# A ConvNeXt-V2 block on one core: convolution in two bursts, another set-up order, Gram and bias add moved

## The chip, the cores and the metric

The kernel runs on one core of one Trainium2 chip. The metric is the device time of that core, in microseconds (us), as the median of several executions. Every run has a state; all runs told here are of state "fast", so no number below compares a disturbed run with an undisturbed one. Engines: PE is TensorE (matmul), ACT is ScalarE, DVE is VectorE, POOL is GpSimd, SP is SyncE. Times inside a kernel come from one profiled execution and count from the start of its span.

## The reference, cut to what matters

```python
# x (1,512,512,96), dw (3,3,96), w1 (96,384), w2 (384,96), gamma, beta (384): bfloat16
out = 0
for i in range(3):
    for j in range(3):
        out += xp[:, i:i+H, j:j+W, :] * dw[i, j]           # depthwise convolution, xp is x padded
h = layernorm(out)                                         # over the 96 channels
h = gelu(einsum('bhwc,ce->bhwe', h, w1))                   # expand 96 -> 384, tanh approximation
gx = sqrt((h * h).sum(axis=(1, 2)) + 1e-6)                 # over ALL pixels
nx = gx / (gx.mean(axis=-1) + 1e-6)
h = gamma * (h * nx) + beta + h
return x + einsum('bhwe,ec->bhwc', h, w2)
```

`gx` needs a sum over the whole picture, so the kernel goes over it twice. The first pass (128 blocks of four rows) makes the convolution, the layer norm, the expansion and the sums of squares. Then comes a short chain that turns the sums into a scale for `w2`. The last stage makes the expansion again in part (`gr`), multiplies by the scaled `w2` and writes the output.

## The kernel before

One slot of the first pass convolves a new block `s` and expands an older block `b`. PE makes the convolution in three bursts of 24 matmuls each. (In the timelines below, `stats` are the 24 matmuls of four columns that sum for the layer norm; the Gram matmuls multiply `gm` by itself, and the diagonal of the result holds sums of squares.) The expansion has six units of 1024 columns: three `pair`, which ACT turns into `gsh`, and three `rest`, which ACT turns into `gm`. All six take their tile of PSUM, the memory that matmuls write to, from one pool of two buffers (`psU`, `bufs=2`), in the order in which they are issued.

```python
def pair(j):                       # two 512-column matmuls, then Gelu on ACT
    U = psU.tile([128, 2, QW], f32, name="U")
    ...
    act.activation(out=gsh[:, :, j, :], in_=U[:], func=ACTF.Gelu_apprx_tanh)

def rest(n):                       # matmuls into 1024 columns, then Gelu on ACT
    U = psU.tile([128, 2, QW], f32, name="U")
    ...
    act.activation(out=gms[b][:, c0:end], in_=Uf, func=ACTF.Gelu_apprx_tanh)

# ... one steady slot, in program order:
for f in bursts[0]: f()            # PE: 24 matmuls of the convolution
pair(0)
pair(1)
squares(0)                         # DVE statistics
for f in bursts[1]: f()
turn_x(s + 2)                      # DVE transposes
pair(2)
rest(0)
squares(1)
for f in bursts[2]: f()
evac()                             # ACT: y_bf, the convolution's result out of PSUM
squares(2)
rest(1)
rest(2)
squares_rest()
stage_stats(b2)                    # PE: 24 tiny matmuls, sums for the layer norm
for f in grams: f()                # PE: 12 Gram matmuls, or 24 for every third block
# ... (loops over lists written on one line here)
```

After the first pass, POOL adds `x` and the constant row `B2c` into `xb`. `B2c` is a copy that DVE makes as the last operation of its scale chain:

```python
m2 = ...                           # DVE: some twenty operations on at most 33 columns follow
...
dve2.tensor_scalar(out=W2s[:, j, :], in0=w2_sb[:, j, :], scalar1=sc[:, j:j + 1], ...)
dve2.tensor_copy(out=B2c[:], in_=B2bc_f[:])
stage_xb(ORDER[0])                 # POOL: xb = xr + B2c
```

## Time and profile before

| | us |
|---|---|
| time, median of three runs | 1584.29 (1584.08 to 1584.38) |
| span of the profiled run | 1588.2 |

The page of the profile gives the busy time of each engine, then the span in 40 equal slices. A digit is the busy share in tenths; the row of PE is shown.

```profile
PE 1483.1 (93%) x23719; PEld 851.6 (54%) x23719; DVE 1147.1 (72%) x2056; ACT 1453.0 (91%) x1307; POOL 1310.6 (83%) x920
...
PE   5798999999999999999999997789999999999998
```

PE and ACT are both nearly full, and that alone says nothing about which one limits. Cutting the span into its stages says more. The following lines are the view by stretches of the kernel before: the stretch, its length, the busy time of each engine with its number of instructions, then the mean granted clock, the DMA share and GB/s. (The granted clock is a share of TensorE's full clock, as the profile records it.) The stretches are the ramp, the steady slots, the tail (expansion without convolution), the bridge (the scale chain) and the last stage.

```profile
0.00:126.17 126.17, 91.26 (x1892) 39.80 (x1893) 77.27 (x189) 73.33 (x69) 48.99 (x56) 0.87 0.48 140
126.17:957.46 831.29, 796.42 (x14010) 396.49 (x14009) 711.81 (x1207) 774.23 (x770) 733.48 (x546) 1.00 0.76 233
957.46:1034.38 76.92, 56.01 (x462) 31.88 (x462) 64.72 (x108) 72.92 (x80) 38.01 (x29) 1.00 0.82 253
1034.38:1055.64 21.26, 15.50 (x146) 10.57 (x146) 12.76 (x45) 11.53 (x14) 8.23 (x5) 0.84 0.33 119
1055.64:1588.20 532.56, 523.93 (x7215) 372.84 (x7211) 280.55 (x507) 521.02 (x378) 481.89 (x287) 1.00 0.99 394
```

The steady stretch has a clock of 1.00, and both PE (96%) and ACT (93%) are nearly always at work in it. In the last stage the DMA share is 0.99, but that does not make DMA its limit: ACT's `gr` follow each other with a single wait, 1.5 us before the first of them, and 83% of the stage's chain that ended last is `gr`, so here ACT sets the length. One steady slot of PE, from the timeline of the kernel before (start, length, engine, line, operation, out<-in, count; idle before and its releaser in brackets):

```profile
707.39 0.44 PE L31 MATMUL SG<-rowsel,y_bf 128*128 128x4 bf16 x12
707.69 0.44 PE L31 MATMUL SG<-rowsel,ysq 128*128 128x4 bf16 x12
707.99 0.83 PE L31 MATMUL SG<-gm 128*128 128x128 bf16 x12
708.75 0.87 PE L31 MATMUL Y<-xT,Wq 64*32 64x512 bf16 x24
709.55 1.11 PE L31 MATMUL U<-ynT,w1p 128*128 128x512 bf16 x4
710.77 0.89 PE L31 MATMUL Y<-xT,Wq 64*32 64x512 bf16 x24
711.60 0.60 PE L31 MATMUL U<-ynT,w1p 128*128 128x512 bf16 x2
712.23 0.60 PE L31 MATMUL U<-w1p,ynT 128*128 128x384 bf16 x4
712.94 0.87 PE L31 MATMUL Y<-xT,Wq 64*32 64x512 bf16 x24
713.74 1.08 PE L31 MATMUL U<-w1p,ynT 128*128 128x128 bf16 x8
```

PE has no pause that the timeline marks: stats, Gram, burst, two pairs, burst, third pair, first rest, burst, the other two rests. ACT in the same slot:

```profile
708.08 1.95 ACT L31 ACTIVATE gm<-U 128x1024 bf16<-128x1024 f32 x2
710.24 3.02 ACT L31 ACTIVATE gsh<-U 128x1024 bf16<-128x1024 f32 x3 [0.22 <-ACT gm L31]
713.16 1.02 ACT L31 ACTIVATE gm<-U 128x1024 bf16<-128x1024 f32 x1
714.06 1.46 ACT L31 ACTIVATE y_bf<-Y 128x1536 bf16<-128x1536 f32 x1
715.39 1.96 ACT L31 ACTIVATE gm<-U 128x1024 bf16<-128x1024 f32 x2
```

ACT makes one `gm` ahead of `y_bf` and two behind it, and it waits 0.22 us for the first pair of a slot. The distance from one `y_bf` to the next is 7.32 us, or 7.87 us for every third block, with 24 Gram matmuls.

### The profile page before, as it was taken

What the parts mean: (1) busy time and instruction counts of PE and PEld (TensorE: products, weight loads), DVE (VectorE), ACT (ScalarE), POOL (GpSimd) and SP (SyncE); (2) the same over time, 40 slices, a digit from 0 to 9 for tenths busy, and PEclk for the clock granted to TensorE, in tenths of its full rate; (3) what the DMA queues carried; (4) which work ended last, traced back from release to release, by engine and by line L of the source; (5) the groups of instructions that cost most, each with busy time, mean ns of one, the idle gap of its engine ahead of it and who ended that gap; (6) DMA issues with size and microseconds to landing.
All of it is one profiled execution on the core that took longest, in us unless ns stands there. A gap on an engine that the chain in (4) does not pass through costs nothing. (4 is left out here: it accounts for less than half of the span.)

```text
span 1588.2 us, 55647 instructions
## 1 busy us (share of the span) xinstructions
PE 1483.1 (93%) x23719; PEld 851.6 (54%) x23719; DVE 1147.1 (72%) x2056; ACT 1453.0 (91%) x1307; POOL 1310.6 (83%) x920
## 2 busy tenths in 40 slices
PE   5798999999999999999999997789999999999998
PEld 1343454444454444444445444457777777777776
DVE  7746888878888888888888888955555555555554
ACT  3777999988999999999999999979999999999998
POOL 0457898897889899898989887369999999899997
PEclk7899999999999999999999999999999999999999
DMA  3549677777778868777877858869999999999995
GB/s 107 164 128 284 210 237 250 220 227 214 252 217 242 264 215 244 231 242 221 250 235 239 245 176 239 249 223 415 410 404 409 410 408 407 411 412 409 412 409 234
DMA packets 186366, 443.67 MB, mean 279 GB/s; under 512 B 33958, under 2 KB 83206, under 8 KB 186118
## 3 DMA queue, kind: packets, MB, share of 16 engines
q1 hardware_dynamic: 171156, 373.10, 69.7%
q0 software_dynamic: 13600, 66.86, 10.7%
q8 instruction: 186, 3.05, 0.8%
q14 instruction: 62, 0.51, 0.1%
q10 hardware_dynamic: 1362, 0.15, 0.1%
HBM read 289.30 MB, written 150.72 MB: 277 GB/s over the span
## 5 line engine op out<-in xcount | busy, mean ns | idle before, releaser
L31 PE MATMUL U<-ynT,w1p 128*128 128x512 bf16 x2166 | 613.4, 382 | 28.5 <-ACT gsh L31 12.1
L31 DVE BATCH_NORM_STATS2 bst<-gsh 128x6 f32<-128x512 bf16 x756 | 468.0, 673 | 142.8 <-ACT gsh L31 142.8
L31 ACT ACTIVATE gr<-U 128x1536 bf16<-128x1536 f32 (+1 forms) x384 | 526.9, 1444 | 15.2 <-PE U L31 9.7
L31 DVE TENSOR_TENSOR o_sb<-O,xb 128x384 bf16<-128x384 f32 x512 | 283.2, 557 | 254.1 <-PE O L31 214.4
L31 POOL TENSOR_TENSOR yn<-y_bf,rbc 128x1536 bf16<-128x1536 bf16 x128 | 397.3, 3107 | 75.8 <-ACT rbc L31 45.0
L31 ACT ACTIVATE gsh<-U 128x1024 bf16<-128x1024 f32 x378 | 370.7, 1023 | 70.5 <-ACT gm L31 44.8
L739 POOL TENSOR_TENSOR xb<-xr,B2c 128x1536 f32<-128x1536 bf16 x128 | 400.8, 3133 | 41.1 <-DVE B2c L31 38.7
L31 ACT ACTIVATE gm<-U 128x1024 bf16<-128x1024 f32 x384 | 379.4, 1039 | 0.1
L31 PE MATMUL Y<-xT,Wq 64*32 64x511 bf16 (+1 forms) x8694 | 326.6, 391 | 29.8 <-issue 3.0
L31 POOL TENSOR_TENSOR ysq<-y_bf 128x1536 bf16<-128x1536 bf16 x114 | 313.5, 2750 | 48.0 <-ACT y_bf L31 47.8
L31 PEld LDWEIGHTS <-w1p 128*128 128x128 bf16 x2166 | 171.7, 98 | 286.7 <-issue 191.7
L31 PEld LDWEIGHTS <-gr 128*128 128x128 bf16 x4584 | 241.5, 98 | 113.1 <-ACT gr L31 13.5
L31 PE MATMUL O<-W2s,gr 128*128 128x96 bf16 x4584 | 279.0, 207 | 5.3 <-DVE o_sb L31 0.8
L31 PEld LDWEIGHTS <-Wq 64*32 64x32 bf16 x9216 | 106.4, 91 | 211.1 <-issue 165.5
L31 ACT ACTIVATE y_bf<-Y 128x1536 bf16<-128x1536 f32 x121 | 176.2, 1456 | 17.1 <-PE Y L31 16.9
L31 DVE STREAM_TRANSPOSE xT<-xin 128x576 f32<-128x576 f32 (+1 forms) x256 | 181.2, 747 | 0.0
L31 PE MATMUL U<-w1p,ynT 128*128 128x384 bf16 (+2 forms) x1032 | 148.4, 273 | 10.7 <-ACT gm L31 4.7
L31 DVE BATCH_NORM_STATS2 bst<-gm 128x6 f32<-128x512 bf16 x252 | 156.8, 677 | 0.7 <-ACT gm L31 0.6
L31 PE MATMUL SG<-gm 128*128 128x128 bf16 x2064 | 135.6, 219 | 0.0
L31 PEld LDWEIGHTS <-ynT 128*128 128x128 bf16 x1032 | 91.3, 97 | 82.4 <-issue 48.1
L31 PEld LDWEIGHTS <-gm 128*128 128x128 bf16 x2064 | 117.3, 97 | 0.9
L714 POOL DMA_DIRECT2D xr<-in_x_dram x128 | 71.0, 555 | 37.9 <-POOL xb L739 34.7
(97 smaller groups left out, 687.8 us busy)
## 6 DMA issues: line engine op xcount, KB each, us to landing
ynT<-yn_dram SPq DMA_DIRECT2D x126, 512.0 KB
xin<-in_x_dram SPq DMA_DIRECT2D x126, 432.0 KB
yn_dram<-yn SPq DMA_DIRECT2D x512, 96.0 KB
ynT<-yn_dram SPq DMA_DIRECT2D x128, 384.0 KB
xr<-in_x_dram POOLq DMA_DIRECT2D x128, 384.0 KB, 6.5
out_dram<-o_sb SPq DMA_DIRECT2D x128, 384.0 KB
g_dram<-gsh SPq DMA_DIRECT2D x126, 384.0 KB
gl<-g_dram SPq DMA_DIRECT2D x84, 384.0 KB
```

The lines of the kernel that those rows point to most:

```text
L31: r = f(*a, **k)
L714: nc.gpsimd.dma_start(out=xr[:], in_=x[0, r0:r0 + GR].rearrange("r w c -> (r w) c").rearrange("(p g) c -> p g c", g=PXP))
L739: nc.gpsimd.tensor_tensor(out=xb[:], in0=grp[q]["xr"][:], in1=B2c[:, None, :].to_broadcast([128, PXP, C]), op=ALU.add)
```

## The change

The intent: fewer switches of PE between convolution and expansion (two bursts instead of three), a set-up that brings the first convolution earlier and gives PE matmuls that nobody reads, in the hope of a higher granted clock, Gram sums that keep PE busy where it used to wait, and a bias add that runs beside the scale chain and not behind it. The core of the diff:

```diff
-    for n in (1, 1, 1, 1):                      # batches of the layer norm in the ramp
+    for n in (1, 1, 2):
@@ set-up
+        for t in yn_ring:                       # six fills, from DVE memset to ACT
+            act.activation(out=t[C:128, :, :], in_=zrow[C:128, None, :]..., func=ACTF.Identity)
+        pool.memset(Wq[:], 0.0)                 # was dve
+        busy(FILL[0])                           # 6, later 24 matmuls that nobody reads
...     # late_setup() of DVE is cut in three: setup_stats(), setup_mlp() at the end of
...     # slot 2, setup_rest() at the end of slot 4
@@ one steady slot
+            bursts = [taps[:2], taps[2:]]
                 for f in bursts[0]:
                     f()
+                if not taps:                    # tail: Gram of the previous block here
+                    for b2 in get("gram"):
+                        if b2 != b:
+                            gram_mms(b2)
                 pair(0)
                 pair(1)
                 squares(0)
                 spread_out()
-                for f in bursts[1]:
-                    f()
                 if s + 2 < NBLK:
                     turn_x(s + 2)
                 pair(2)
-                rest(0)
                 squares(1)
...
-                for f in bursts[2]:
+                for f in bursts[1]:
                     f()
                 if evac:
                     evac()
+                rest(0)
                 squares(2)
                 rest(1)
                 rest(2)
@@ behind the first pass
-        LEAD = UPB
+        LEAD = 2 * UPB                          # six gr ahead of the chain, not three
         advance(LEAD, PRE)
+        stage_xb(ORDER[0])                      # ahead of the chain
...
-        dve2.tensor_copy(out=B2c[:], in_=B2bc_f[:])
-        stage_xb(ORDER[0])
@@ stage_xb
-                                    in1=B2c[:, None, :].to_broadcast([128, PXP, C]), op=ALU.add)
+                                    in1=B2bc_f[:, None, :].to_broadcast([128, PXP, C]), op=ALU.add)
```

## The prediction

> **What bounds the kernel now.** Span 1588.2 us, three stages (timeline, stretches).
> - Ramp, to about 125 us: set-up, granted clock 0.57 to 0.66 between 20 and 60 us, first expansion (ACT gsh) at 53.2 us, steady expansions from 126 us.
> - Steady blocks, to 957 us. ACT does three gsh (0.93 us pitch), three gm (0.93) and y_bf (1.34): 7.0 us a block. Block periods are 7.22 us, and 7.85 for every third block (24 Gram matmuls, not 12); mean with hiccups 7.55 over 107 blocks. Not ACT alone: at each boundary it waits 0.2 or 0.83 us (PE comes late with the first pair).
> - Tail without convolution (5.6 us a block), a bridge (1040 to 1056; ACT busy 10.3 of 20 us), then expansions gr back to back on ACT (1.38 us each, 99% busy).

> **The loop that matters.** Expansions rotate over two PSUM tiles; the sixth (last rest) overwrites the tile that the first gm reads. So: first gsh starts -> first gm ends (3.83 us) -> last rest (0.53) -> stats (0.61) -> Gram (0.76 or 1.43) -> conv burst (0.80) -> first pair until its gsh starts (0.69). Sum 7.22 or 7.89: the measured periods.

> **What the change does to it.** New order, PE: two bursts, three pairs, third burst, three rests, stats, Gram; ACT: gsh x3, y_bf, gm x3.
> 1. y_bf precedes the first gm: +1.34 us in the loop.
> 2. The second burst precedes the first pair: three back-to-back bursts take 2.78 us, so +0.98.
> The saved switch between convolution and expansion (0.1 to 0.3 us of PE) falls where PE waits for the first gm anyway. Period 9.5 and 10.2 us: +2.3 on some 110 blocks (part hidden in hiccups): **+246 us**.
> 3. Tail: Gram of the previous block precedes the next pairs and needs the last gm, so ACT waits Gram plus 0.76 us: +1.45 us on 14 blocks, less 1.4 us of Gram at the end: **+19 us**.
> 4. Ramp: DVE loses 5.4 us of ynT memsets and half the Wq copies; the second convolution no longer waits until 21.7 us[...]. But ACT fills ynT, six writes of 1.9 us (estimate from the 1536-element ysq, 1.48 us), so the first y_bf stays near 18 us. First gsh near 42 us; then early blocks are slower and one more conv-only slot (3.6 us) comes. Net **-9 us**.
> 5. Bridge: six expansions before the scale chain, not three, fill 2.6 us of ACT wait; xb (3.1 us) leaves the chain; but they delay the tot matmul by 1.8 us, and the longer lead leaves four more output groups at the end. Net **-4 us**.

> **Prediction:** 1584.3 + 246 + 19 - 9 - 4 = about **1836 us**, 8 in 10 between 1790 and 1880. Faster by over 2%: 0.02; within 2%: 0.02; slower by over 2%: 0.96.

> **Right if:** period 9.4 to 10.3 us; ACT idle 2 to 2.5 us before each first gsh; PE idle about 1.5 us before each last rest, released by the first gm; PE busy 75 to 85% in the steady stretch, clock 1.00; tail blocks 7.05/7.75 us; first gsh at 36 to 46 us; last stage unchanged.
> **Wrong if:** the last rest need not wait for the first gm; PE gaps lower the clock (slower still); the ramp gains tens of us.

## The result, and the profile after

| kernel | median, us | lowest to highest | runs |
|---|---|---|---|
| before | 1584.34 | 1584.08 to 1587.6 | 4 |
| after | 1899.84 | 1898.48 to 1900.22 | 4 |

The ratio of after to before is 1.1984, 95% interval 1.1963 to 1.2005. A ratio here is the mean time of one kernel's fast runs over that of the other's of the same rounds, so it is not quite the ratio of the medians that are quoted. The direction was predicted, and the time lies 64 us above the predicted 1836 and above the upper end, 1880.

The same lines of the page of the kernel after:

```profile
PE 1528.9 (81%) x23749; PEld 905.5 (48%) x23749; DVE 1141.3 (60%) x2026; ACT 1451.8 (76%) x1312; POOL 1314.1 (69%) x927
...
PE   6777777777777777777777777776699999999998
```

ACT and DVE do the same work within 0.6%, and PE is busy 46 us longer although the change adds only the thirty fill matmuls. Part of the work must have run slower. The view by stretches, cut at the same events:

```profile
0.00:125.91 125.91, 92.02 (x1850) 41.48 (x1851) 63.12 (x158) 80.73 (x71) 47.10 (x50) 0.89 0.45 132
125.91:1251.27 1125.36, 846.50 (x14096) 448.43 (x14095) 715.63 (x1209) 771.71 (x773) 744.22 (x561) 0.95 0.58 175
1251.27:1342.21 90.94, 60.27 (x475) 33.12 (x474) 64.81 (x108) 72.86 (x79) 32.66 (x26) 0.98 0.66 213
1342.21:1365.90 23.69, 10.88 (x72) 5.89 (x71) 19.57 (x40) 11.21 (x12) 10.87 (x6) 0.81 0.34 112
1365.90:1898.40 532.50, 519.24 (x7263) 376.61 (x7260) 278.13 (x511) 515.30 (x378) 479.29 (x285) 1.00 0.98 392
```

Subtracting the lengths gives the ledger:

| stage | before | after | difference | predicted |
|---|---|---|---|---|
| ramp | 126.17 | 125.91 | -0.3 | -9 |
| steady | 831.29 | 1125.36 | +294.1 | +246 |
| tail | 76.92 | 90.94 | +14.0 | +19 |
| bridge | 21.26 | 23.69 | +2.4 | -4 |
| last stage | 532.56 | 532.50 | -0.1 | 0 |
| sum | 1588.2 | 1898.4 | +310.2 | +252 |

(The cuts in both kernels are the first `gsh` of the steady slots, the first `gsh` after the last `y_bf`, the last expansion into `resg`, which is the `gsh` of the two blocks kept on chip, and the seventh `gr`. The steady stretch of after holds one more slot of convolution alone, 4 to 5 us, which the prediction had booked under the ramp.) The steady stage is nearly all of it. PE in two of its slots in the kernel after:

```profile
704.74 0.60 PE L32 MATMUL U<-w1p,ynT 128*128 128x256 bf16 x4 [1.60 <-ACT gm L32]
...
705.78 0.83 PE L32 MATMUL SG<-gm 128*128 128x128 bf16 x12
706.54 1.86 PE L32 MATMUL Y<-xT,Wq 64*32 64x512 bf16 x48
708.33 1.04 PE L32 MATMUL U<-ynT,w1p 128*128 128x512 bf16 x4
710.10 0.59 PE L32 MATMUL U<-ynT,w1p 128*128 128x512 bf16 x2 [0.73 <-ACT gsh L32]
...
714.25 0.60 PE L32 MATMUL U<-w1p,ynT 128*128 128x256 bf16 x4 [1.60 <-ACT gm L32]
...
715.28 2.72 PE L32 MATMUL SG<-gm 128*128 128x128 bf16 x24
717.93 2.23 PE L32 MATMUL Y<-xT,Wq 64*32 64x512 bf16 x48
```

The first slot is what the prediction described: the last rest waits 1.60 us for the first `gm`, and then stats, 12 Gram matmuls (0.83), two bursts (1.86) and the first pair follow each other. In the second slot 24 Gram matmuls take 2.72 us. They took 1.50 us in the kernel before (at 700.09 us of its timeline), and the two bursts take 2.23 and not 1.86 us. ACT, in the same stretch of the kernel after, shows what this costs:

```profile
709.02 2.85 ACT L32 ACTIVATE gsh<-U 128x1024 bf16<-128x1024 f32 x3 [2.50 <-issue]
711.83 1.45 ACT L32 ACTIVATE y_bf<-Y 128x1536 bf16<-128x1536 f32 x1
713.18 2.85 ACT L32 ACTIVATE gm<-U 128x1024 bf16<-128x1024 f32 x3
720.79 2.85 ACT L32 ACTIVATE gsh<-U 128x1024 bf16<-128x1024 f32 x3 [4.75 <-issue]
```

(`<-issue` means that the profile shows nothing that the engine waited for.) ACT idles 2.50 us ahead of a normal slot, as predicted (2 to 2.5), and 4.75 us ahead of a third one. `y_bf` follows `y_bf` at 9.5, 9.5 and 11.75 us. Predicted were 9.5 and 10.2. The reason is the granted clock, the third column from the right in the view by stretches, here in pieces of 3.4 us of the kernel after:

```profile
708.40:711.80 3.40, 2.57 (x31) 0.82 (x32) 1.72 (x3) 2.78 (x3) 3.40 (x2) 1.00 0.41 102
711.80:715.20 3.40, 1.80 (x30) 1.25 (x29) 3.40 (x8) 3.40 (x5) 3.40 (x2) 1.00 0.46 134
715.20:718.60 3.40, 3.40 (x49) 2.84 (x54) 1.76 (x3) 0.83 (x1) 3.40 (x2) 0.52 0.74 209
718.60:722.00 3.40, 2.54 (x45) 0.78 (x30) 0.16 (x1) 1.21 (x2) 1.29 (x1) 0.98 0.93 290
```

The clock falls to half for one such piece, just when the longest run of PE work begins. The piece before it has PE busy for 1.80 of 3.40 us, and 0.6 us of that are the tiny stats matmuls of four columns. By the clock records of the trace, falls begin at 715.3, 746.0, 776.8, 807.5, 838.2 and 868.9 us, 30.72 us apart, which is three slots (9.5 + 9.5 + 11.7). The records of this trace and of the kernel before hold two values only, 1.00 and 0.50. Between 200 and 1180 us of after there are 32 falls of 3.41 us each, and from 285.2 to 1237.6 us one begins every 30.72 us, nine times 3.413 us. PE need not be idle for anything like that long: in the steady stage its longest pause is 1.61 us.

The bridge lengthened. DVE in the scale chain of the kernel before:

```profile
1042.48 0.19 DVE L31 TENSOR_TENSOR m<-m,mv 128x33 f32<-128x33 f32 x1
1042.71 0.19 DVE L31 TENSOR_TENSOR m<-m,npx 128x33 f32<-128x33 f32 x1
...
1043.36 0.17 DVE L31 TENSOR_SCALAR gi<-ssq 128x3 int32<-128x3 int32 x1
```

The same three operations in the kernel after:

```profile
1349.49 3.00 DVE L32 TENSOR_TENSOR m<-m,mv 128x33 f32<-128x33 f32 x1
1352.52 3.04 DVE L32 TENSOR_TENSOR m<-m,npx 128x33 f32<-128x33 f32 x1
...
1356.01 3.69 DVE L32 TENSOR_SCALAR gi<-ssq 128x3 int32<-128x3 int32 x1
```

What POOL did in those microseconds, and what ACT then waited for, both from the timeline of the kernel after:

```profile
1349.33 6.18 POOL L774 TENSOR_TENSOR xb<-xr,B2bc_f 128x1536 f32<-128x1536 bf16 x2 [48.15 <-DVE junk L32]
1355.45 1.09 POOL L749 DMA_DIRECT2D xr<-in_x_dram  x2
1356.56 3.11 POOL L774 TENSOR_TENSOR xb<-xr,B2bc_f 128x1536 f32<-128x1536 bf16 x1
```

```profile
1350.08 5.61 ACT L32 ACTIVATE gr<-U 128x1024 bf16<-128x1024 f32 x6 [2.27 <-PE U L32]
1365.90 1.45 ACT L32 ACTIVATE gr<-U 128x1536 bf16<-128x1536 f32 x1 [10.22 <-PE U L32]
```

Two operations on 33 columns took as long as a `xb` of POOL beside them, and one on three columns took 3.69 us; it began 0.55 us before its `xb`, while POOL was at its line of DMA issues. The second and third ended within 0.1 us of the end of a `xb` (1355.56 against 1355.51, 1359.70 against 1359.67). The chain from the first `m` to the last `W2s` took 14.3 us, against 4.95 us before. How an operation of DVE is held up by a `xb` these traces do not show: the first two have two input tiles and the third has one, and the third was held although it started before its `xb`. That POOL is the cause is tested below (e9_combined against e12_b2c_gate).

### The profile page after: what moved, and what is told of

Same layout as the page of the kernel before. It is cut to its first block, busy times and chain, and to the rows that moved or that the text cites. A ratio compares the mean times of both kernels' runs of the same rounds, so it can differ in the third digit from the quotient of the medians.

```text
span 1898.4 us, 55685 instructions
## 1 busy us (share of the span) xinstructions
PE 1528.9 (81%) x23749; PEld 905.5 (48%) x23749; DVE 1141.3 (60%) x2026; ACT 1451.8 (76%) x1312; POOL 1314.1 (69%) x927
## 5 line engine op out<-in xcount | busy, mean ns | idle before, releaser
L32 PE MATMUL U<-ynT,w1p 128*128 128x512 bf16 x2166 | 590.8, 381 | 105.4 <-ACT gsh L32 95.8
L32 ACT ACTIVATE gsh<-U 128x1024 bf16<-128x1024 f32 x378 | 359.8, 1024 | 379.3 <-issue 354.8
L774 POOL TENSOR_TENSOR xb<-xr,B2bc_f 128x1536 f32<-128x1536 bf16 x128 | 400.8, 3133 | 60.1 <-DVE junk L32 48.2
L32 ACT ACTIVATE gm<-U 128x1024 bf16<-128x1024 f32 x384 | 365.2, 1033 | 0.0
L32 PE MATMUL Y<-xT,Wq 64*32 64x511 bf16 (+1 forms) x8694 | 335.0, 403 | 32.0 <-issue 3.1
L32 PEld LDWEIGHTS <-w1p 128*128 128x128 bf16 x2166 | 180.2, 98 | 334.8 <-issue 222.6
L32 PE MATMUL U<-w1p,ynT 128*128 128x384 bf16 (+2 forms) x1032 | 155.5, 272 | 188.5 <-ACT gm L32 184.6
L32 PE MATMUL O<-W2s,gr 128*128 128x96 bf16 x4584 | 256.9, 206 | 9.0 <-DVE o_sb L32 8.6
L32 PE MATMUL SG<-gm 128*128 128x128 bf16 x2064 | 180.2, 256 | 9.4 <-ACT gm L32 7.4
L32 ACT ACTIVATE y_bf<-Y 128x1536 bf16<-128x1536 f32 x121 | 175.6, 1451 | 10.2 <-PE Y L32 10.2
L32 PEld LDWEIGHTS <-gm 128*128 128x128 bf16 x2064 | 155.8, 117 | 14.3 <-ACT gm L32 11.4
```

What stands on the lines that cost most here:

```text
L32: r = f(*a, **k)
L774: nc.gpsimd.tensor_tensor(out=xb[:], in0=grp[q]["xr"][:], in1=B2bc_f[:, None, :].to_broadcast([128, PXP, C]), op=ALU.add)
```

## The experiments

**The theory.** The order inside the slot makes nearly all of the loss, in two parts. First, the loop of dependences grows: `y_bf` stands ahead of the first `gm` (+1.34 us), and the second burst stands ahead of the first pair (+0.98 us). Second, the PE pause of 1.60 us that this opens makes the granted clock fall. **The rivals**: the set-up, the Gram order or the batches take part in the steady loss; or the long third periods have another cause than the clock.

Each group of runs shared runs of the kernel before on its own chip; their medians were 1591.1, 1588.1, 1586.0, 1588.6 and 1587.4 us. Most groups have two runs of a kernel, so differences below about 5 us are not settled by them. In the diffs, calls that stand on several lines are joined with semicolons, and loops over a list are cut.

**1. The old order back, all else as after.**

```diff
-                for f in bursts[0]:
+                for f in taps[:1]:
                     f()
                 pair(0); pair(1); squares(0); spread_out()
+                for f in taps[1:2]:
+                    f()
...
                 pair(2)
+                rest(0)
                 squares(1)
...
-                for f in bursts[1]:
+                for f in taps[2:]:
                     f()
...             # evac()
-                rest(0)
```

> The changed kernel with only the order inside a block put back (one burst, two pairs, second burst, third pair, first rest, third burst with y_bf, two rests); ramp, tail and bridge stay as changed. Theory (the loop through y_bf and the second burst costs the steady stretch): block periods return to 7.2 and 7.85 us, first steady gsh to last y_bf shrinks by about 290 us, clock 1.00 there, time about 1605 us (1595 to 1620). Rival (set-up, batching or the clock state left by the new ramp slow the blocks): block periods stay above 8 us and the time above 1650 us.

Measured: 1604.38 us (1603.97 to 1604.79), ratio 1.010. The periods are 7.32 and 7.87 us, the mean 7.59 us a block with the extra slot of convolution, and the clock is 1.00 in the steady stage. The order is the loss; the rest of the change costs some 1%.

**2. The order alone, in the kernel before.** The edit is the reverse one: nothing else of the change is in.

```diff
-for f in bursts[0]: f()
+for f in taps[:2]: f()
 pair(0); pair(1); squares(0); spread_out()
-for f in bursts[1]: f()
 turn_x(s + 2); pair(2)
-rest(0)
 squares(1)
-for f in bursts[2]: f()
+for f in taps[2:]: f()
 evac()
+rest(0)
 squares(2); rest(1); rest(2)
```

> The kernel before with nothing changed but the order inside the block: both early bursts ahead of the pairs, y_bf ahead of the gm. Theory, that the order alone makes the loss and the drop of the granted clock: y_bf periods 9.5, 9.5, 11.75 us as in the kernel after, clock 0.50 for some 3.5 us in every third block, tail and bridge as in before, time 1870 to 1890 us. Rival, that part of the 294 us of the steady stage or the clock drops come from another part of the change (set-up, Gram ahead, batches): 1850 us or less, or periods without the 11.75.

Measured: 1884.46 us (1881.84 to 1887.08), ratio 1.1877; periods 9.5, 9.5 and 11.7 us from 500 us on (less regular before), and the same 24 Gram matmuls of 2.72 us. Together with the first experiment this closes the sum from both sides: the order alone adds 18.8%, the rest alone 1.0%, and both 19.8%.

**3. Which half of the order.** The first kernel keeps the two bursts and puts only `rest(0)` back ahead of the third burst, so that one `gm` precedes `y_bf` again. The second puts only the second burst back behind `pair(1)`.

```diff
# e2_rest_first
                 pair(2)
+                rest(0)
...
-                rest(0)                        # behind evac()
# e3_three_bursts
-                for f in bursts[0]:
+                for f in taps[:1]:
                     f()
                 pair(0); pair(1); squares(0); spread_out()
+                for f in taps[1:2]:
+                    f()
...
-                for f in bursts[1]:
+                for f in taps[2:]:
                     f()
```

> The changed kernel with the first rest put back ahead of the third burst, so y_bf follows the first gm again; two bursts stay ahead of the first pair. Theory (both terms in the loop): y_bf leaves the loop, periods 8.2 and 8.9 us if the clock holds, time about 1700 us; with a clock drop in every third block up to 1755 us. Rival (the two adjacent bursts alone slow the block, y_bf's place is harmless): periods stay 9.5 us and more, time about 1900 us.

> The changed kernel with the second burst put back after the second pair; y_bf stays ahead of the first gm. Theory: the second burst leaves the loop, periods 8.55 and 9.2 us if the clock holds, time about 1740 us; with a clock drop in every third block up to 1795 us. Rival (y_bf's place alone is the cause): no gain from this edit, about 1900 us.

Measured: e2_rest_first takes 1699.64 us (1697.37 to 1701.92), ratio 1.070, periods 8.24, 8.24 and 8.9 us, clock 1.00. So the second burst costs 0.92 us a slot, where 0.98 was predicted. e3_three_bursts takes 1833.06 us (1831.65 to 1834.48), ratio 1.154. Its undisturbed slots have 8.71 and 9.37 us, so `y_bf` costs 1.39 us, where 1.34 was predicted. (In one kernel the two cost a little less than their sum: 9.49 - 7.32 = 2.17 us, where 2.32 was predicted.) But its clock is 0.92 between 200 and 900 us, and 48 of 101 intervals are more than 0.3 us longer than the loop asks. The expectation missed the time: it allowed for a fall of the clock in every third block, up to 1795 us, and the falls came in nearly every second. Both terms of the loop are shown; what the clock does to them is another matter.

**4. Is it the clock?** Eight matmuls of zeros, 128x384, are added to the Gram sums ahead of the last rest, where PE only waits. They change no result, and they fit into the pause: by the timeline, eight take 1.46 us of PE, and 0.26 to 0.30 us of the pause are left.

```diff
                 rest(1)
+                for _ in range(8 if taps else 0):
+                    pe.matmul(SG[:, 2 * NS:], lhsT=zrow[:, :128], rhs=zrow[:, :NCH * 128], start=False, stop=True,
+                              skip_group_check=True)
                 rest(2)
```

> The changed kernel with eight 128x384 matmuls on zeros, added into the Gram sums (nothing changes in them), ahead of the last rest, where PE waits 1.6 us for the first gm. Theory of the clock (the pause lets the clock fall to 0.5 in every third block, which makes that block 11.7 us and not 10.2): clock 1.00 over the steady stretch, third blocks near 10.2 us, others still 9.5 us, time about 1843 us (1835 to 1860). Rival (third blocks are long for their 24 Gram matmuls and order alone, or zeros do not count as activity): third blocks stay at 11.7 us or grow, time 1895 us or more.

> e3_three_bursts (1833.1 us, clock 0.90 to 0.93, periods 8.7 to 10.9 us) with eight extra matmuls of zeros (128x384) added to the Gram sums ahead of the last rest of each block. Theory, that the clock drops alone put e3_three_bursts above the 1740 us that its loop gives: clock 1.00 in the steady stage, periods 8.7 and 9.37 us, mean about 8.95 us, time 1750 to 1770 us. Rival, that its long periods come from another wait: time stays above 1800 us although the clock reads 1.00.

Measured: e4_warm_fill, which is the kernel after with the fill, takes 1839.05 us (1837.98 to 1840.11), ratio 1.1577. Its clock is 1.00 from 200 to 900 us and its periods are 9.49, 9.50 and 10.17 us, the predicted ones. e11_three_bursts_fill, which is e3_three_bursts with the fill, takes 1751.77 us (1750.52 to 1753.02) and has periods of 8.71 and 9.37 us at clock 1.00: 81 us less than without the fill. More work on PE made both kernels faster, so the long periods are the clock's. In the kernel after the clock costs 1899.84 - 1839.05, about 61 us (the two ran on different chips; by their ratios it is about 64 us).

**5. How little fill is enough, and where.** Because the prediction's error was the clock, this was taken further: four, two and one fill matmul a slot in place of eight, and two fills behind the last rest, where the pause stays as it is.

> The kernel after with four fill matmuls of zeros a block in the pause ahead of the last rest, where e4_warm_fill had eight. Pause about 0.95 us, against 0.26 to 0.30 with eight and 1.60 with none. Theory, that the clock falls where PE did too little in a stretch of some 3.4 us, so a dose has a limit: with half the pause filled no falls, periods 9.5, 9.5, 10.17 us, clock 1.00, time 1835 to 1845 us. Rival, that any pause near 1 us in the wrong phase suffices: falls stay, a period of 11 us or more in some blocks, time 1860 us or more.

> The same with two fill matmuls a block, pause about 1.3 us. Theory of a limit: the falls come back in part or whole, time 1850 to 1900 us. Rival, that any filling breaks the phase: no falls, clock 1.00, time 1835 to 1845 us as with eight.

> The kernel after with one fill matmul a block in the pause, pause about 1.45 us. If the limit lies between one and two fills: the falls are back in part or whole, 1855 to 1900 us. If the kernel after lies right at the limit: no falls, clock 1.00, third period 10.17 us, 1838 to 1845 us. No odds given for either.

> The kernel after with two fill matmuls a block behind the last rest instead of ahead of it: they are in the loop and cost about 0.33 us a block (two of 0.16 us), some 36 us; the pause stays at 1.60 us. Theory, that PE's work in the stretch of 3.4 us before the fall counts: no falls, periods 9.8, 9.8, 10.5 us, clock 1.00, 1870 to 1885 us. Rival, that the length of the pause counts: falls stay, a period of 11 us or more in every second or third block, 1905 us or more.

Measured (a "long" interval is one `y_bf` to the next that exceeds the loop's own period by over 0.3 us, counted between 200 and 1180 us):

| kernel | fill | pause before the last rest, us | long intervals | falls in the clock records | time, us |
|---|---|---|---|---|---|
| after | none | 1.55 to 1.61 | 32 of 94 | 32 | 1899.84 |
| e15_fill_one | 1 in the pause | 1.39 to 1.45 | 16 of 97 | 15 | 1870.25 |
| e14_fill_two | 2 in the pause | 1.22 to 1.28 | 1 of 100 | 0 | 1841.99 |
| e13_fill_four | 4 in the pause | 0.88 to 0.95 | 1 of 100 | 1 | 1841.38 |
| e4_warm_fill | 8 in the pause | 0.25 to 0.31 | 2 of 100 | 0 | 1839.05 |
| e16_fill_after_rest | 2 behind the rest | 1.54 to 1.61 | 13 of 95 | 12 | 1902.97 |

(The kernel before has 4 of 100 by the same count, from other hiccups.) The line of e14_fill_two that answers to the 2.72 us above:

```profile
715.28 1.50 PE L32 MATMUL SG<-gm 128*128 128x128 bf16 x24
```

Two fills, 0.49 us of PE's busy time, end the falls; the theory of a limit had expected them to come back at that dose, and that part of the expectation fell. With one fill they come in half as many slots. So in this loop the falls end between one and two such matmuls. The last run was to tell the pause's length from the work in the stretch, and by its time it told neither: the pause stayed as long and the falls became fewer (12, not 32), but they did not end.

A stretch laid at the worst place of a normal slot of after is filled to about 0.32 by the same count, and one fill adds 384 columns, 0.16 us or 0.05 of a stretch, where it falls into it. That the columns streamed in such a stretch count, and not the length of the pause as such, is the author's estimate. It fits the two traces, and the 12 falls of e16 against 32 at the same pause; no run tests it alone. The time of e16 is no gain, since its fills stand in the loop (9.8 us a normal slot, not 9.5).

**6. The parts outside the slot.** All on top of e1_old_order, so that the order's loss is out of the way.

```diff
# e6_gram_back: Gram of the tail again at the end of its own slot
-                if not taps:
-                    for b2 in get("gram"):  ...
-                    if taps or b2 == b:
-                        gram_mms(b2)
+                    gram_mms(b2)
# e7_mlp_setup_later
-            if s == 2:
+            if s == 3:
                 setup_mlp()
# e8_no_fill
-FILL = (6, 24)
+FILL = (0, 0)
# e5_xb_back: only the call of stage_xb(ORDER[0]) goes back behind W2s
```

> The kernel of e1_old_order with the Gram matmuls of the tail put back behind the rests of the next block. Theory (in the tail ACT waits for Gram, which waits for the last gm): tail periods fall from 6.8 to 5.6 us (6.3 after every third block), ACT's wait of 1.2 us before each first gsh is gone or down to 0.1 and 0.7, the time falls by 12 to 15 us. Rival (the tail is held by the normalised rows that come in by DMA): periods stay above 6.5 us, the time falls by less than 4 us.

> The kernel of e1_old_order with the set-up of the expansion weights one slot later (after the fourth convolution, not the third). Theory (its PSUM tile, freed by DVE only after the scale chain of block 1, keeps the fourth convolution waiting): that convolution starts near 27 us and not 32, ACT's wait of 7.5 us before the fourth y_bf shrinks below 2 us, the first gsh comes at 43 to 46 us and not 50.6, and the steady blocks begin 3 to 8 us earlier. Rival (the ramp is set by the chain of norms and DMA writes from block 4 on, so early gains are lost again): the first gsh is early but the steady blocks begin within 2 us of before, no gain in time.

> The kernel after with the old order in the block (as e1_old_order, 1604.4 us) and both groups of readerless fill matmuls taken out. Theory, that the fill matmuls buy nothing because the first y_bf waits for ACT's six ynT fills until 17.45 us whatever the clock: within 2 us of e1_old_order, 1602 to 1607 us, ratio to before 1.008 to 1.012, first gsh within 1 us of 51 us. Rival, that the fills warm the clock through the ramp: 5 us or more slower, first gsh at 55 us or later.

> The kernel of e1_old_order (the changed kernel with the old order inside a block, 1604 us) with the first bias add on POOL (xb) put back behind the scale chain; the sums are the same. Theory (each xb of 3.1 us on POOL holds up a DVE instruction of the chain; three of them took 2.99, 3.03 and 3.69 us, and a chain from first m to last W2s lasts 14.3 us): those three take 0.2 us again, the chain 5.5 to 6.5 us, the seventh gr starts 6 to 8 us earlier against the last gm, the time falls by 4 to 8 us against e1_old_order. Rival (the six expansions ahead of the chain or the Gram end delay it, POOL does not matter): the three instructions stay long or another wait takes their place, the time within 1.5 us of e1_old_order.

Measured:

| kernel | time, us | ratio to before, 95% interval |
|---|---|---|
| e1_old_order | 1604.38 | 1.0100 (1.0019 to 1.0181) |
| e6_gram_back | 1586.58 | 0.9994 (0.9961 to 1.0028) |
| e7_mlp_setup_later | 1593.90 | 1.0041 (1.0013 to 1.0069) |
| e8_no_fill | 1603.36 | 1.0123 (1.0080 to 1.0167) |
| e5_xb_back | 1600.59 | 1.0079 (1.0051 to 1.0106) |

- Gram: in the tail of after ACT waits 1.19 us ahead of every first `gsh`, and a block takes 6.8 us (one of the waits is 3.77 us, at a fall of the clock). With Gram back the waits are gone except 0.67 us in every third block, and blocks take 5.6 or 6.27 us, as in before. The gain of 17.8 us is somewhat more than the tail's own 14, and two runs of e1 do not settle the difference.
- Set-up: in after `setup_mlp` stands at the end of slot 2. Its second group of matmuls writes the PSUM tile that DVE still has to read for `w1p`, and DVE does so only behind the layer-norm chain of block 1, until 31.66 us. PE waits 4.80 us for that, and the fourth convolution stands behind it, from 32.04 us on: ACT idles 7.46 us ahead of its `y_bf` (8.23 us in e1_old_order). One slot later the wait is 1.77 us, that `y_bf` starts at 30.92 and not at 36.56 us, and the late ramp comes 8.3 us earlier (below). The expectation had been 3 to 8. By the medians of two chips the kernel gains 10.5 us, but the intervals in the table overlap.
- Fill matmuls in the ramp: no effect that these runs show. The granted clock between 20 and 40 us is 0.66 without them and 0.60 with them (e1_old_order), and 0.83 and 0.80 between 40 and 60 us. The first `y_bf` starts at 17.74 us without them and 17.46 us with them, because ACT is busy until then with its own six fills of `ynT` (10.90 us in the timeline of after).
- The bias add: a miss of the edit. Only the call was moved, but POOL is a queue of its own and started `xb` beside the chain all the same: 3.00, 3.04 and 3.69 us again, and ACT idle 10.22 us. What had held POOL back in the kernel before was not the order of the calls; it was the data, the `B2c` copy behind `W2s`. (The time is 3.8 us under e1_old_order by the medians of two chips, which decides nothing.)

**7. The combinations, and POOL against DVE.** e9_combined takes the old order, Gram back, the later set-up and the moved call. e12_b2c_gate adds to this the copy that gates POOL.

```diff
+        B2c = ....tile([128, C], f32, name="B2c")
-                                    in1=B2bc_f[:, None, :].to_broadcast([128, PXP, C]), op=ALU.add)
+                                    in1=B2c[:, None, :].to_broadcast([128, PXP, C]), op=ALU.add)
+        dve2.tensor_copy(out=B2c[:], in_=B2bc_f[:])     # behind W2s
```

> All four at once: old order inside a block, Gram of the tail back, bias add behind the chain, expansion set-up one slot later; what is left of the change is the rest of the set-up, the fill matmuls, two blocks in the third batch, the fused chain, and six expansions ahead of the scale chain. Theory (the parts are in different stretches and add up): 1604 - 6 - 13 - 4 = about 1581 us (1574 to 1588), 0 to 0.7% faster than before on the same chip. Rival (the stretches hand their gains on to a common wait, DMA or the clock): 1590 us or more.

> e9_combined (1580.5 us, ratio 0.9954) with the bias add reading B2c again, the copy that DVE makes after W2s, as in before, so that POOL cannot start xb beside DVE's scale chain. Theory, that xb on POOL beside the chain holds DVE up (3.00, 3.04 and 3.69 us for operations of 0.2 us): these operations are back at 0.2 us, the chain from the first m to the last W2s takes 5 to 6.5 us and not 14.3, ACT idles 2 to 4 us and not 10.2 before the seventh gr, time 1571 to 1576 us, ratio 0.989 to 0.993. Rival, that DVE is slow there for another reason, or that the last stage takes the gain back because its DMA has the lead: within 1.5 us of e9_combined.

Measured: e9_combined takes 1580.48 us (1579.24 to 1581.93), ratio 0.9954 (0.9927 to 0.9981). e12_b2c_gate takes 1575.16 us (1574.54 to 1579.95), ratio 0.9934 (0.9903 to 0.9966). The DVE lines of e12_b2c_gate:

```profile
1029.03 0.20 DVE L32 TENSOR_TENSOR m<-m,mv 128x33 f32<-128x33 f32 x1
1029.26 0.20 DVE L32 TENSOR_TENSOR m<-m,npx 128x33 f32<-128x33 f32 x1
...
1029.91 0.17 DVE L32 TENSOR_SCALAR gi<-ssq 128x3 int32<-128x3 int32 x1
```

With POOL out of the way the three operations are back at 0.2 us: POOL's `xb` was the cause. The chain takes 6.7 us (a little more than the 5 to 6.5 expected), the seventh `gr` starts at 1036.80 and not at 1045.39 us, 8.6 us earlier. Of these, 4 us are given back afterwards: the rest of the span is 537.2 us here and 533.2 us in e9_combined. Why is not tested; in that stretch 35% of the chain that ended last is POOL's `xb`, against 22% in e9_combined. The two kernels ran on different chips and their ratios overlap, so the size of the gain in time (some 5 us by the medians) is not settled; that the chain is shorter is. Both are a little faster than the kernel before, by an interval that excludes 1, and well inside 2%.

## Why the prediction was right or wrong

- **Slower, and by the order in the slot: right.** Both terms of the loop came out nearly as computed: 0.92 us for the second burst (predicted 0.98), 1.39 us for `y_bf` (predicted 1.34), 2.17 us for both in one kernel (predicted 2.32). The base of the loop, 7.22 us, lay 0.1 us under the measured 7.32. The normal slots of after have the predicted 9.5 us, with ACT idle 2.50 us and PE idle 1.60 us where it said.
- **The step that failed** is the third block, "Period 9.5 and 10.2 us: +2.3 on some 110 blocks", with "clock 1.00" among what should be seen. The period was 11.75 us, because the clock falls to 0.50 there for 3.4 us. With two to eight fill matmuls in the pause it is 10.17 us and the time 1839 to 1842 us. The prediction named this as a danger ("PE gaps lower the clock (slower still)") and gave it no microseconds. It had the pause's length, 1.5 us, and did not ask how much PE does in the microseconds around it: in before and after the clock fell behind each of the 33 stretches of 3.41 us that were filled with columns to 0.333 or less, and behind none of the 505 that were filled to 0.391 or more (an estimate, worked out from the two traces under experiment 5), though in the steady stage of after PE was never idle for longer than 1.61 us. The missing term measures about 61 us, against the 64 us by which the time exceeded 1836.
- **That the rest sums up is partly luck.** e4_warm_fill, without the falls, comes within 3 us of 1836, but its terms do not. Ramp and bridge were off by 8.7 and 6.4 us on the slow side, the tail by 5 us on the fast side, and the steady stage without the falls, about 294 - 61 = 233 us (an estimate from the ledger and e4_warm_fill), was 13 us under its 246. Most of that is the loop term: 2.17 us on 107 blocks is 232 us.
- **Ramp, -9 predicted, -0.3 measured.** That "the first y_bf stays near 18 us" held (17.45). "First gsh near 42 us" did not (50.97; before 53.15): the order of the set-up made ACT wait 7.46 us for the fourth convolution, shown by e7_mlp_setup_later. With that wait mended, the first `gsh` of a late slot of the ramp comes at 109.74 and not at 118.05 us (e7_mlp_setup_later against e1_old_order). The fill matmuls bought nothing that e8_no_fill could show (clock 0.66 between 20 and 40 us without them, 0.60 with them).
- **Bridge, -4 predicted, +2.4 measured.** "xb (3.1 us) leaves the chain" did happen, and it stands beside the chain instead and holds DVE up for 9.2 us (3.00 + 3.04 + 3.69 less 0.55). The prediction costed an engine that moves off the path, and not what it does to the engine that stays on it. e12_b2c_gate shows it.
- **Tail, +19 predicted, +14.0 measured.** The mechanism was right (ACT waits for the Gram matmuls in every block, 1.19 us); the term was mis-sized, since 1.45 us on 14 blocks was assumed and the blocks lengthen by 6.8 - 5.6 = 1.2 us, less for every third.
- **Last stage unchanged: right** in after (532.50 against 532.56 us), though ACT no longer works through it without a wait: 8.8 us of waits follow the seventh `gr`. Why the length stays the same no run shows.

## What to carry to other kernels

Where tiles rotate through few buffers, the order of issue is a loop of dependences: write it as a sum of durations from the trace before moving one line, and both sides of a proposed order can be priced to 0.15 us a slot. Then look at the pause that the new order opens on PE, and at what stands beside it: here 1.60 us of pause in a slot of 9.5 us, next to 0.6 us of matmuls of four columns, cost a further 61 us by the clock (e4_warm_fill), and two matmuls of zeros in that pause brought nearly all of it back (1841.99 us, not 1899.84). And before moving work of POOL beside a chain of short DVE operations, price what the one does to the other: one `xb` of 3.1 us turned a DVE operation of 0.2 us into one of 3.0 us, and only a data dependence, not the place of the call, kept them apart.
